# A transformer block on one core: a new fixed order for the same instructions, with 75 of them on another engine

## The chip, the cores and the metric

The kernel runs on one core of a Trainium2 chip. The core has five engines that run side by side, each with its own queue that it works off in order: TensorE for matmuls (PE in the profile, PEld for its weight loads), VectorE (DVE), ScalarE (ACT), GpSimd (POOL) and SyncE (SP), which here only issues DMAs. Engines wait for one another by semaphores. The metric is the device time of one execution in microseconds; a kernel's figure is the median of its runs.

## The reference

One block of a conditioned transformer on 2048 tokens of width 640, in bfloat16. Six rows of 640 numbers come from `silu(c) @ w_mod`: shift, scale and gate for either half.

```python
h = _layernorm(x) * (1 + ca) + sa
x = x + ga * A(h)        # attention: 32 heads of 20, causal, window of 256 keys, then @ wo
h = _layernorm(x) * (1 + cb) + sb
x = x + gb * B(h)        # (sigmoid(h @ w_gate) * (h @ w_up)) @ w_down, inner width 1536
```

## The kernel before

The 2048 tokens are worked in 8 chunks of 256 tokens (two blocks of 128 rows). For each chunk `a` these steps follow one another:

- `ln1`: load x, layer norm statistics on DVE (L776, L778), the inverse root on POOL (L781, L783), the normalised x on DVE (L796) or POOL (L793). It is transposed to hT by PE for chunks 0 to 2 and by a DMA on SP (L803) for the rest; hT then gets scale and shift (the "modulation", L811 on ACT, L812 on DVE or POOL; L857, L858 where it is evacuated from PE's transpose).
- `qkv`: hT times wqkv, in runs of five matmuls of 480 columns into one PSUM bank M; the result is cast out by ACT (L893) or DVE (L894) into stg (queries and keys) or V. stg is transposed to QT and KT, by PE in chunks 0 and 1, by DMAs on SP after that.
- `attention`: in each of two halves of the heads, five sets of scores (three in chunk 0). A set writes the one score tile S, four PSUM banks; ACT takes exp of it into E (L1015), and S can be written again only then. POOL sets the entries outside the window to zero (L1040). Then a burst of PV matmuls (E times V, L669) into a pair of M banks, and `norm` on DVE (L1082 to L1091): transpose, divide by the sum, transpose back. The result goes through DRAM (`doc`) and comes back as oT. A PV burst is issued together with a score set of the next half.
- `outproj`: oT times wo, added to x (L1164), a second layer norm, and h2T by DMA transposes with modulation.
- `mlp`: for six pairs of 128 columns each, ten matmuls for the gate (wg) and ten for the up projection (wu), each into one M bank; tanh on ACT (L1209, out: sig) frees the gate's bank, the product on DVE (L1211, out: hh) the other. Then hh times wd ("down"), added to x (L1230), and out.

The gates ga and gb are not applied to the results: wo and wd are scaled by them (L1253, L1192, out<-in `wd<-wd,gbc`) once the gate's row has been spread over the partitions through DRAM (`gate<-gq`, `gbc<-gate`).

All matmuls of these steps stand on two helper lines: L668 for full tiles, L669 for scores and PV, which use parts of the array.

What sets the order: the build first lists 2121 operations (`Prog.op`), each with its dependencies. The list `PRIO` then gives each operation a number. `schedule` goes through the operations in the order of these numbers; a number's remainder by 5 names the engine:

```python
for o in sorted(self.ops, key=lambda x: x.prio):
    e = ENGS[o.prio % 5]      # ("pe", "act", "dve", "pool", "sp")
```

So `PRIO` fixes each engine's queue. Tiles (buffers) are handed out on the way: of a pool's free buffers an operation takes the one that comes free earliest by the durations written in the program. M has 4 banks, S one, E five buffers. `emit` then puts a semaphore wait ahead of every operation whose inputs or buffer come from another engine.

Of the kernel before, what the change touches and what calls it, by code (L numbers as in the profile page):

```python
# [25 lines left out]
SWITCH = 0.095  # L26
ENGATTR = {"pe": "tensor", "act": "scalar", "dve": "vector", "pool": "gpsimd", "sp": "sync"}
ENGS = ("pe", "act", "dve", "pool", "sp")
OVERLAP = {"pe": 0.0, "act": 0.085, "dve": 0.075, "pool": 0.045, "sp": 0.0}
# [52 lines left out]
class Prog:  # L82
# [69 lines left out]
    def schedule(self):  # L152


        free = {e: START for e in ENGS}
        bw = 0.0
        lastturn = False
# [4 lines left out]
        pemode = 0  # L162
        portend = 0.0
        freed = {}

        def slot_time(pool, s):
            ten = pool.tenant[s]
            if ten is None:
                if not all(x.done for x in pool.init[s]):
                    return None  # L170
                return max([x.end + x.lat for x in pool.init[s]], default=0.0)
            return None if ten.left else freed[ten]

        def take(t, s):
            ten = t.pool.tenant[s]
            t.prev = list(t.pool.init[s]) if ten is None else list(ten.rel)
            t.slot = s
            t.pool.tenant[s] = t

        for o in sorted(self.ops, key=lambda x: x.prio):  # L180
            assert all(d.done for d in o.deps), o.tag
            e = ENGS[o.prio % 5]
            assert e in o.engs, (o.tag, e)
            o.eng = e
            st = max([o.tmin, free[e] + (SWITCH if e == "pe" and o.mode != pemode else 0.0)]
                     + [d.end + (0.0 if d.eng == "pe" and e == "pe" else d.lat) for d in o.deps])
            if o.isdma and e == "sp":
                st = max(st, bw - QMAX)
            for t in o.tiles:
                if t.slot is None:  # L190
                    step = 1 if t.mate is None else 2
                    best = None
                    for s in range(0, len(t.pool.tenant), step):
                        rts = [slot_time(t.pool, s + k) for k in range(step)]
                        if None not in rts and (best is None or max(rts) < best[0]):
                            best = (max(rts), s)
                    assert best is not None, (o.tag, t.name)
                    if t.mate is None:
                        take(t, best[1])
                    else:  # L200
                        take(t, best[1] + t.odd)
                        take(t.mate, best[1] + 1 - t.odd)
                for x in t.prev:
                    st = max(st, x.end + x.lat)
            if e == "dve" and o.port:
                st = max(st, free["pool"])
            elif e == "pool":
                st = max(st, portend)
            o.start = st
            if e == "pe":  # L210
                pemode = o.mout
            dur = o.dur[e]
            free[e] = st + dur - OVERLAP[e]
            if e == "dve" and o.port:
                portend = free[e]
            if o.isdma:
                turn = o.dlat > 3.0
                if e == "sp" and bw - st > 2.0:
                    free[e] += 0.35 if o.dur[e] > 1.0 else 0.1
                bw = max(st + o.dlat, bw + (MIXED if turn != lastturn and bw > st + o.dlat else 0.0)) + o.work  # L220
                lastturn = turn
                o.end = max(bw - 0.83, st + dur)
                s = rr
                rr = (rr + 1) % NDMA
                dmacnt[s] += 16
                o.key, o.val = f"d{s}", dmacnt[s]
                if dmalast[s] is not None:
                    o.deps.append(dmalast[s])
                dmalast[s] = o
            else:  # L230
                o.end = st + dur
            order[e].append(o)
            o.done = True
            for t in o.tiles:
                t.left -= 1
                if t.left == 0:
                    last = {}
                    for x in t.ops:
                        if x.isdma:
                            last[x] = x  # L240
                    for e2 in ENGS:
                        xs = [x for x in t.ops if x.eng == e2 and not x.isdma]
                        if xs:
                            last[e2] = max(xs, key=lambda x: x.start)
                    t.rel = list(last.values())
                    freed[t] = max(x.end + x.lat for x in t.rel)
        self.order = order
        self.span = max(o.end for o in self.ops)
# [88 lines left out]
def c_pe(n):  # L337
# [3 lines left out]
PE_EPS = 0.14  # L341
PRIO = [
# [142 lines left out]
QMAX = 4.5  # L485
# [821 lines left out]
```

## Time and profile before

| | |
|---|---|
| median of 3 runs | 325.76 us (325.64 to 326.33) |
| span of the profiled execution, first to last instruction | 324.3 us |
| median less this span | 1.46 us |
| TensorE busy | 317.3 us, 98% of the span |
| VectorE, ScalarE, GpSimd busy | 211.8, 212.3, 187.2 us |
| granted TensorE clock | 1.000 |

The profiled execution is one of its own; no device time beside its span is listed for it, so the 1.46 us stand for what lies around a span.

How to read it: the rows name the line, the engine, the operation, the tile written and the tiles read, the shape and the count. In a timeline each row has its start and its length in us, like instructions in a row being merged into one (xcount), and in brackets the idle time of the engine just before, with the instruction that ended it. A matmul's shown length holds the time it spends in the array, so lengths of neighbours overlap; what one more matmul costs is seen from longer rows: a row of 15 matmuls of 480 columns takes 3.21 us and one of 9 takes 2.00, so one more costs 0.2. SPq and ACTq are DMA issues, whose length is that of issuing.

### The profile page before, as it was taken

What the parts mean: (1) busy time and instruction counts of PE and PEld (TensorE: products, weight loads), DVE (VectorE), ACT (ScalarE), POOL (GpSimd) and SP (SyncE); (2) the same over time, 40 slices, a digit from 0 to 9 for tenths busy, and PEclk for the clock granted to TensorE, in tenths of its full rate; (3) what the DMA queues carried; (4) which work ended last, traced back from release to release, by engine and by line L of the source; (5) the groups of instructions that cost most, each with busy time, mean ns of one, the idle gap of its engine ahead of it and who ended that gap; (6) DMA issues with size and microseconds to landing.
All of it is one profiled execution on the core that took longest, in us unless ns stands there. A gap on an engine that the chain in (4) does not pass through costs nothing.

```text
span 324.3 us, 11594 instructions
## 1 busy us (share of the span) xinstructions
PE 317.3 (98%) x4872; PEld 222.7 (69%) x4873; DVE 211.8 (65%) x424; ACT 212.3 (65%) x316; POOL 187.2 (58%) x276
## 2 busy tenths in 40 slices
PE   8999999989999999999999999999999999999997
PEld 3564545446776568765776467877786788787885
DVE  5797898778687959674477475837463769264332
ACT  1899985889876687788687867786767764011120
POOL 5128869976668694847585939382939691012100
DMA  7998799989891383824405394340213032202101
GB/s 249 371 333 299 165 269 180 200 137 183 260 164 22 83 109 77 152 61 101 85 22 82 97 103 110 92 69 5 81 40 88 3 79 53 76 20 64 40 2 40
DMA packets 71694, 37.85 MB, mean 117 GB/s; under 512 B 45274, under 2 KB 70362, under 8 KB 71642
## 3 DMA queue, kind: packets, MB, share of 16 engines
q1 hardware_dynamic: 69616, 35.31, 48.3%
q10 hardware_dynamic: 2026, 1.80, 2.1%
q8 instruction: 38, 0.62, 0.8%
q14 instruction: 14, 0.11, 0.1%
HBM read 21.30 MB, written 5.25 MB: 82 GB/s over the span
## 4 chain that ended last, share of the span: by engine, by line
PE 73%; DMA 2%; SPq 2%; DVE 1%; POOL 1%; issue 0%; DVEq 0%
PE M L668 61%; PE S L669 6%; PE M L669 5%; DMA gbc<-gate 2%; SPq L803 2%; DVE wd L1192 1%; POOL x L793 0%; POOL st L788 0%; DVE hh L1211 0%; POOL E L1040 0%; DVE x L1230 0%; DVEq L310 0%
## 5 line engine op out<-in xcount | busy, mean ns | idle before, releaser
L1040 POOL TENSOR_SCALAR_AFFINE_SELECT E<-E 128x512 bf16<-128x512 bf16 (+1 forms) x176 | 142.6, 836 | 68.7 <-ACT E L1015 67.0
L1015 ACT ACTIVATE E<-S 128x512 bf16<-128x512 f32 (+2 forms) x184 | 150.9, 878 | 47.4 <-PE S L669 46.5
L668 PE MATMUL M<-wqkv,hT 128*128 128x480 bf16 (+1 forms) x340 | 73.9, 355 | 0.6 <-ACT hT L846 0.5
L668 PE MATMUL M<-h2T,wu 128*128 128x256 bf16 x480 | 68.0, 273 | 0.5 <-DVE hh L1211 0.5
L668 PE MATMUL M<-h2T,wg 128*128 128x256 bf16 x480 | 67.8, 273 | 0.0
L668 PE MATMUL M<-wd,hh 128*128 128x320 bf16 (+2 forms) x396 | 58.1, 295 | 0.0
L1209 ACT ACTIVATE sig<-M 128x512 f32<-128x512 f32 x48 | 28.9, 602 | 44.1 <-PE M L668 41.7
L1211 DVE SCALAR_TENSOR_TENSOR hh<-sig,M 128x512 bf16<-128x512 f32 x48 | 32.4, 681 | 37.1 <-ACT sig L1209 24.0
L668 PEld LDWEIGHTS M<-h2T,wu 128*128 128x128 bf16 x480 | 45.9, 98 | 8.4 <-issue 1.2
L668 PEld LDWEIGHTS M<-h2T,wg 128*128 128x128 bf16 x480 | 45.7, 98 | 7.1
L668 PEld LDWEIGHTS M<-wqkv,hT 128*128 128x128 bf16 x340 | 30.1, 98 | 27.6 <-DMA wqkv<-in_A_wqkv_dram 1.6
L668 PEld LDWEIGHTS M<-wd,hh 128*128 128x128 bf16 x396 | 36.8, 98 | 14.3 <-DVE hh L1211 0.2
L669 PEld LDWEIGHTS S<-QT,KT 20*64 20x64 bf16 (+1 forms) x1856 | 19.9, 100 | 21.3 <-ACT E L1015 12.0
L1230 DVE TENSOR_TENSOR x<-M,x 128x320 bf16<-128x320 f32 (+2 forms) x33 | 15.6, 476 | 27.2 <-PE M L668 27.2
L669 PE MATMUL S<-QT,KT 20*64 20x256 bf16 (+5 forms) x1856 | 32.1, 228 | 1.2 <-ACT E L1015 1.2
L776 DVE BATCH_NORM_STATS2 st<-x 128x6 f32<-128x320 bf16 x64 | 28.6, 477 | 2.3 <-DMA x<-in_A_x_dram 1.9
L1082 DVE STREAM_TRANSPOSE T<-M 128x512 f32<-128x512 f32 x32 | 21.5, 698 | 9.2 <-PE S L669 8.0
L668 PE MATMUL M<-wo,oT 128*128 128x320 bf16 x160 | 25.4, 299 | 0.0
L669 PE MATMUL M<-E,V 128*32 128x128 bf16 (+1 forms) x960 | 22.8, 246 | 0.8 <-ACT E L1015 0.4
L781 POOL TENSOR_SCALAR st<-st 128x2 f32<-128x2 f32 x16 | 3.7, 234 | 33.8 <-DVE st L778 33.6
L669 PEld LDWEIGHTS M<-E,V 128*32 128x32 bf16 x960 | 19.2, 97 | 5.3 <-issue 2.9
L1091 DVE STREAM_TRANSPOSE On<-Tn 128x1024 bf16<-128x1024 bf16 x16 | 19.8, 1240 | 0.3
(77 smaller groups left out, 240.2 us busy)
## 6 DMA issues: line engine op xcount, KB each, us to landing
x<-in_A_x_dram SPq DMA_DIRECT2D x23, 160.0 KB, 2.3
doc<-On SPq DMA_DIRECT2D x56, 40.0 KB
wd<-in_B_w_down_dram SPq DMA_DIRECT2D x4, 480.0 KB
wd<-in_w_mod_dram SPq DMA_DIRECT2D x5, 320.0 KB
wqkv<-in_A_wqkv_dram SPq DMA_DIRECT2D x4, 400.0 KB
wu<-in_w_mod_dram SPq DMA_DIRECT2D x5, 320.0 KB
oT<-doc SPq DMA_DIRECT2D x8, 192.0 KB, 2.5
out_dram<-x SPq DMA_DIRECT2D x9, 160.0 KB
```

The source lines that it names most:

```text
L668: return e.matmul(o, l, r, start=st, stop=sp, skip_group_check=True)
L669: return e.matmul(o, l, r, start=st, stop=sp, tile_position=tp, skip_group_check=True)
L776: A("dve", lambda e, g, bi=bi, j=j: e.bn_stats(v(bi * 12 + j * 6, 6), src[bi].ap[:, j * 320:(j + 1) * 320]), 0.48, reads=[src[bi].r()], wr ...
L781: A("pool", lambda e, g: e.tensor_scalar(v(28, n), var(), EPS, None, op0=ALU.add), 0.2, reads=[st.r(("m", bi)) for bi in range(n)], writes ...
L803: return e.dma_start_transpose(dst(), src())
L1015: A("act", lambda e, eng: e.activation(dst(), src(), ACT.Exp, scale=SM_SCALE), c_act(n), reads=[Sp.r()], writes=[E.r(key)], prio=3, tag=f" ...
L1040: A("pool", lambda e, eng: e.affine_select(rows(dst), rows(src), pattern=[[0, 8], [sign, n]], compare_op=ALU.is_ge, fill=0.0, base=base, c ...
L1082: A("dve", lambda e, g, h=h: e.transpose(T1.ap[:, 512 * h:512 * h + 512], X[h].ap), 0.694, reads=[X[h].r()], writes=[T1.r(h)], prio=3.5, t ...
L1091: A("dve", lambda e, g: e.transpose(On.ap[:], Tn.ap[:]), 1.22, reads=[Tn.r()], writes=[On.r()], prio=4, tag=f"tr2_{a}")
L1209: A("act", lambda e, g, pg=pg, sg=sg: e.activation(sg.ap[:], pg.ap[:], ACT.Tanh, scale=0.5), c_act(512), reads=[pg.r()], writes=[sg.r()], ...
L1211: A("dve", lambda e, g, pu=pu, sg=sg, f0=f0: e.scalar_tensor_tensor(out=hh.ap[:, f0:f0 + 2, :], in0=sg.ap[:].rearrange("p (a b) -> p a b", ...
L1230: A("dve", lambda e, g, ps=ps, bi=bi, c0=c0, n=n: e.tensor_tensor(x1[bi].ap[:, c0:c0 + n], ps.ap[:, 0:n], x1[bi].ap[:, c0:c0 + n], op=ALU. ...
```

## The change

`PRIO` gets new numbers, and a list `SLOTS` names the buffer of each of 709 tiles, in place of the choice by durations. `schedule` loses the model of durations that chose the buffers. No operation is added, removed or altered.

```diff
-                    step = 1 if t.mate is None else 2
-                    best = None
...
+                    s = SLOTS[tiles[t]] if SLOTS else 0
+                    ten = t.pool.tenant[s]
...
 PRIO = [
-    23, 28, 258, 8, 43, 33, 958, 18, 1448, 38, 3, 507, 513, 72, 67, 48, 53, 58, 76, 84, 101, 99, 144, 149, 154, 159,
+    23, 28, 258, 8, 43, 33, 718, 18, 1218, 38, 3, 507, 513, 72, 67, 48, 53, 58, 76, 84, 101, 99, 144, 149, 154, 159,
...
+SLOTS = [
+    0, 1, 3, 2, 0, 0, 0, 1, 0, 2, 0, 1, 3, 0, 1, 2, 3, 0, 0, 1, 0, 2, 0, 0, 3, 1, 0, 4, 5, 1, 3, 2, 2, 3, 2, 1, 3,
...
```

Sorted by their numbers, the lists say this. The first 140 operations are the same, on the same engines. SP's queue of 193 operations is the same, the 18 DMAs on ACT's queue keep their order, and the 79 operations with scores or PV keep theirs among themselves on PE. Of PE's 907 operations 613 have another place in its queue, by at most 19 places. 75 operations change engine: evacuations of queries, keys and values between ACT and DVE (20 to DVE, 15 to ACT), evacuations of QT, KT and hT between the same two, modulations among ACT, DVE and POOL, and one scaling of wd from POOL to DVE. By engine, before and after: PE 907 and 907, ACT 333 and 331, DVE 424 and 433, POOL 264 and 257, SP 193 and 193.

Some stretches, decoded (number of matmuls in brackets; a number behind a name is the chunk):

```
PE, gaps ahead of the 12th to the 15th of the 79 operations with scores or PV (| is such an operation)
before  q3 k3 (15) | v2 v3 (9)     | v3 q2 v2 (15) | q2 k2 v2 (11) PV
after   q3 k3 (12) | q3 v3 v2 (12) | v3 q2 v2 (13) | q2 v2 k2 (13) PV

PE, the five gaps between scores that end with the second PV of chunk 1
before  q3 wo k3 (14) | k3 q3 wo (11) | q3 wo (10) | q4 (12) | q4 (8) PV
after   q3 wo    (10) | wo       (15) | q3 k3 (10) | q4 (12) | q4 (8) PV

PE, gaps with the first MLP (u: up, g: gate, first chunk), up to the first PV of chunk 2
before  k4 v4 u(4) | g u (20) | g u (24) | g u (44) PV
after   v4 k4 u(2) | g u (20) | g u (20) | g u (52) PV

PE, first PV of chunk 0
before  score | q1 q1 qtr q1 | PV | q1 qtr q1 | score
after   q1 q1 qtr q1 | score | PV | q1 q1 qtr | score

DVE, around the second gate's scaling of wd
before  hh, wd, wd, wd, wd, hh, hh, hh, wd, wd, wd, wd
after   hh, stg, V, wd, hh, wd, statistics, hh, wd, wd, hh, wd, statistics, wd

DVE, ahead of the second PV of chunk 0 (chunk 2's hT, chunk 1's QT)
before  hT, gq, T, QT, QT, hT, hT, hT, gq, T
after   hT, gq, T, QT, hT, hT, T, hT, gq      (the other QT and one hT on ACT)

DVE, second layer norm of chunk 0
before  x, x, stg(4), stg(4), divide
after   x, stg(4), stg(4), x, divide          (the second stg's matmuls: before the 1st score of chunk 2, now behind it)

ACT, exps (e) of chunk 1's last two score sets and chunk 2's first
before  e e | hT hT hT hT e e | stg(4) e e
after   stg(3) e e | hT hT e hT hT e | stg(4) e e
```

More of the change, by code (lines that the diff above doesn't have):

```diff
@@ L152, in schedule @@
     def schedule(self):
-        free = {e: START for e in ENGS}
-        bw = 0.0
-        lastturn = False
         order = {e: [] for e in ENGS}
@@ L161, in schedule, with number @@
         rr = 0
[L162 to L178, printed above, removed]
+        tiles = {}
+        def number(t):
+            if t is not None and t not in tiles:
+                tiles[t] = len(tiles)
+                number(t.mate)
+        for o in self.ops:
+            for t in o.tiles:
+                number(t)
         for o in sorted(self.ops, key=lambda x: x.prio):
@@ L184, in schedule @@
             o.eng = e
[L185 to L188, printed above, removed]
             for t in o.tiles:
                 if t.slot is None:
-                    step = 1 if t.mate is None else 2
-                    best = None
[L193 to L215, printed above, removed]
-            if o.isdma:
[L217 to L223, printed above, removed]
-                rr = (rr + 1) % NDMA
[L225 to L231, printed above, removed]
+                    s = SLOTS[tiles[t]] if SLOTS else 0
@@ new lines, in schedule @@
+                    ten = t.pool.tenant[s]
+                    assert ten is not None or all(x.done for x in t.pool.init[s]), (o.tag, t.name)
+                    assert ten is None or ten.left == 0, (o.tag, t.name)
+                    t.prev = list(t.pool.init[s]) if ten is None else list(ten.rel)
+                    t.slot = s
+                    t.pool.tenant[s] = t
+            if o.isdma:
+                dmacnt[rr] += 16
+                o.key, o.val = f"d{rr}", dmacnt[rr]
+                if dmalast[rr] is not None:
+                    o.deps.append(dmalast[rr])
+                dmalast[rr] = o
+                rr = (rr + 1) % NDMA
@@ L237, in schedule @@
                     last = {}
[L238 to L244, printed above, removed]
+                    for x in sorted(t.ops, key=lambda x: x.prio):
+                        last[x if x.isdma else x.eng] = x
                     t.rel = list(last.values())
-                    freed[t] = max(x.end + x.lat for x in t.rel)
         self.order = order
-        self.span = max(o.end for o in self.ops)
     def emit(self):
@@ L338, in c_pe @@
     return max(n, 64) / 2400.0 + 0.0027
-PE_EPS = 0.14
 PRIO = [
[3 rows of a table removed]
[3 rows of a table added]
     92, 87, 187, 237, 242, 247, 253, 263, 272, 267, 280, 275, 290, 300, 305, 286, 317, 296, 322, 311, 376, 357, 386,
[1 row of a table removed]
[1 row of a table added]
     541, 495, 501, 665, 677, 480, 485, 491, 565, 570, 576, 545, 551, 630, 652, 525, 555, 561, 625, 660, 681, 685,
[111 rows of a table removed]
[111 rows of a table added]
+]
+SLOTS = [
[20 rows of a table added]
 ]
@@ L466 @@
 DSAFE = 1.5
-START = 0.8
-PORTLAG = 0.05
-MIXED = 0.55
 NPB = 0
```

3 lines of the change are left out of this document (removed), and 247 rows, old and new, of tables (PRIO, SLOTS).

## The prediction

> **What bounds the kernel now.** I read the page first, then TensorE's busy time in seven stretches, then the timelines of the stretches where it is idle.
>
> ```profile
> span 324.3 us, 11594 instructions
> PE 317.3 (98%) x4872; PEld 222.7 (69%) x4873; DVE 211.8 (65%) x424; ACT 212.3 (65%) x316; POOL 187.2 (58%) x276
> ...
> q8 instruction: 38, 0.62, 0.8%
> ```
>
> ```profile
> 0.00:10.30 10.30, 8.35 (x76) 1.00 0.82 272
> 10.30:36.00 25.70, 25.62 (x297) 1.00 0.91 301
> 36.00:61.00 25.00, 24.48 (x421) 1.00 1.06 211
> 61.00:72.00 11.00, 9.43 (x177) 1.00 0.84 164
> 72.00:92.00 20.00, 19.49 (x339) 1.00 1.04 223
> 92.00:270.00 178.00, 177.99 (x3134) 1.00 0.39 76
> 270.00:322.20 52.20, 51.91 (x450) 1.00 0.14 39
> ```
>
> Each row gives a stretch, its length, TensorE's busy time and its clock, which is full throughout. Length less busy time is idle time. The first 10.3 us lose 1.95 us, but belong to the 140 operations that keep their places. After 92 us nothing is lost until the last matmul (the 0.29 us in the last row lies behind it). In between: 0.08 + 0.52 + 1.57 + 0.51 = **2.68 us**. TensorE does the same 4872 matmuls in both kernels, so 2.68 us is all that a new order can take out of visible idle time, while in the 230 us after 92 it can only add some. The change is a bet on the stretch from 36 to 92 us.
>
> [...]
>
> **The change, place by place.** The diff alters no instruction's work. All 193 operations on SP's queue keep their order, and so do the DMAs on ACT's; so do the 79 score and PV operations among themselves on PE. What moves are 613 of 907 PE operations by up to 19 places between those, evacuations and modulations among ACT, DVE and POOL, and the buffer that each tile gets. The idle places are these (bracket: idle time ahead, and what ended it):
>
> ```profile
> 38.23 0.84 PE L669 MATMUL M<-E,V 128*32 128x256 bf16 x32 [0.35 <-DVE hT L858]
> ...
> 42.99 3.21 PE L668 MATMUL M<-wqkv,hT 128*128 128x480 bf16 x15
> 46.13 0.43 PE L669 MATMUL S<-QT,KT 20*64 20x256 bf16 x24
> 46.49 2.00 PE L668 MATMUL M<-wqkv,hT 128*128 128x480 bf16 x9
> 48.66 0.43 PE L669 MATMUL S<-QT,KT 20*64 20x256 bf16 x24 [0.17 <-ACT E L1015]
> ...
> 58.92 0.41 PE L669 MATMUL S<-QT,KT 20*128 20x64 bf16 x32
> ...
> 61.60 0.43 PE L669 MATMUL S<-QT,KT 20*64 20x256 bf16 x24 [0.27 <-ACT E L1015]
> ...
> 64.13 0.43 PE L669 MATMUL S<-QT,KT 20*64 20x256 bf16 x24 [0.30 <-ACT E L1015]
> ...
> 67.91 0.43 PE L669 MATMUL S<-QT,KT 20*64 20x256 bf16 x24 [0.42 <-ACT E L1015]
> ...
> 70.48 1.50 PE L669 MATMUL M<-E,V 128*32 128x128 bf16 x64 [0.42 <-ACT E L1015]
> ...
> 86.54 1.25 PE L668 MATMUL M<-h2T,wu 128*128 128x256 bf16 x10 [0.51 <-DVE hh L1211]
> ```
>
> *Place 1, 86.5 us.* The gate for wd lands late, and DVE, in order, stands behind it:
>
> ```profile
> 77.92 5.14 DMA gbc<-gate
> ```
>
> ```profile
> 80.35 0.69 DVE L1211 SCALAR_TENSOR_TENSOR hh<-sig,M 128x512 bf16<-128x512 f32 x1 [0.94 <-ACT sig L1209]
> 83.16 2.65 DVE L1192 TENSOR_TENSOR wd<-wd,gbc 128x640 bf16<-128x640 bf16 x4 [2.12 <-DMA gbc<-gate]
> 85.72 1.27 DVE L1211 SCALAR_TENSOR_TENSOR hh<-sig,M 128x512 bf16<-128x512 f32 x2
> ```
>
> Before, four scalings of wd (2.65 us, 0.66 each) run ahead of the second hh product; the bank that this frees is what PE waits for, from 86.03 to 86.54. After, one scaling stands ahead of that product: 83.16 + 0.66 = 83.8. Its tanh ends at 83.93 (83.34 + 0.59, row below), so it ends near 84.6 instead of 86.4. PE asks no sooner: the 90 matmuls of projection and MLP that lie ahead of the waiting one from chunk 4's keys on are 68 and 22, split by the last score there; after, 62 and 28. The wait has a margin of 86.0 − 84.6 = 1.4 us and goes: **−0.51**. It returns only if the gate lands over 1.4 us later. The scalings pushed back are needed by the down projection alone, which follows the whole first MLP.
>
> *Place 2, 38.2 us.* PV waits for a bank that DVE's hT evacuations free. Before, two QT evacuations stand ahead of those on DVE; after, one, the other having gone to ACT, and one hT evacuation each way changes engine. One such QT evacuation is 2.1/3 = 0.7 us:
>
> ```profile
> L894 DVE CAST QT<-M 128x512 bf16<-128x512 f32 x3 | 2.1, 686 | 1.1 <-PE M L668 1.1
> ```
>
> That covers the 0.35. But ACT's copy now runs behind the exps there, next to a score that reads QT. Between 0 and −0.35 I take **−0.2**.
>
> *Place 3, 48.7 us.* Three of the 15 matmuls ahead of the score at 46.13 move behind it (12 and 12 instead of 15 and 9, 0.2 us each by the quoted rows). A stg evacuation leaves ACT just ahead, so the earlier score finds ACT free. 0.6 us of work covers 0.17 of wait: **−0.17**.
>
> *Place 4, 58 to 70.5 us.* Over half of the idle time: 0.27 + 0.30 + 0.42 + 0.42 = 1.41 us. S has one buffer, so each score waits for the exps of the one before. ACT:
>
> ```profile
> 59.49 2.06 ACT L1015 ACTIVATE E<-S 128x512 bf16<-128x512 f32 x4 [0.72 <-PE S L669]
> 62.14 1.94 ACT L1015 ACTIVATE E<-S 128x512 bf16<-128x512 f32 x2 [0.59 <-PE S L669]
> 63.97 2.07 ACT L811 ACTIVATE hT<-hT,mA 128x256 bf16<-128x256 bf16 x4
> 65.93 1.92 ACT L1015 ACTIVATE E<-S 128x1536 bf16<-128x1536 f32 x2
> ...
> 83.34 0.59 ACT L1209 ACTIVATE sig<-M 128x512 f32<-128x512 f32 x1
> ```
>
> Score to score is 61.60 − 58.92, then 2.53, 3.78, 2.57 us: exps of 1.94 to 2.06, about 0.6 of hand-over, and in the third gap four modulations (2.07). The new order leaves all four on ACT, only mixed with the exps, and PE the same 55 matmuls spread otherwise over the five gaps that end at 70.48. Two extra evacuations on ACT fall into its idle 0.72 and 0.59. A loop that ACT closes isn't shortened: **0**, between −0.3 (an evacuation fewer beside the modulations) and +0.5 (one that misses its gap).
>
> *Place 5, 25 to 30 us.* A score of chunk 0 goes four operations back, to directly ahead of the first PV: one change of PE's mode fewer (161 for 162). Its second exp now waits for PV, which frees an E buffer:
>
> ```profile
> 28.29 1.02 ACT L1015 ACTIVATE E<-S 128x1024 bf16<-128x1024 f32 x1 [0.29 <-PE M L669]
> ```
>
> After, it waits for the first exp (1.02) of the later score instead, some 0.2 us longer at most, with projections as cover. **0**, between −0.2 and +0.3.
>
> *The rest, 92 to 322 us.* PE waits for nothing here before. What could make it wait is the same loop, if too few matmuls lie between two scores. The seven thinnest gaps before hold about ten 480-column matmuls (2.0 to 2.1 us at 0.2 us each); the new order has three such gaps, so it is no tighter. **0**, between 0 and +1.5, nearer to 0 for this reason.
>
> **Sum:** −0.51 − 0.2 − 0.17 = −0.88 us, span 323.4. The shown runs have a median of 325.76 (325.64 to 326.33), 1.46 over the profiled span; start and end are unchanged, so I keep 1.46: **324.9 us**.
>
> **Rivals.**
>
> *A. Nothing measurable.* (0.2%, 0.65 us, is about what a measurement of this kernel tells from no change.) PE that gets to the loop at 56 us sooner still needs QT and KT from SP's unchanged queue, and waits there instead; places 2 and 3 are given back. A new wait of 0.2 somewhere in 230 us does the rest: −0.51 + 0.2, 325.4. Against it: before 56 us PE waits for no such transfer. The change's own aim may also be empty: instruction fetches are 0.62 MB in 38 packets, 0.8% of the DMA engines' time, and no PE wait is put down to them.
>
> [...]
>
> *B. Slower: h2T and the gate come late.* The second normalised x of the first chunk moves behind two stg evacuations on DVE, and the matmuls of the second of them behind the score at 67.91. Those end near 67.91 + 0.43 + five times 0.2 = 69.4, the evacuation (0.7) at 70.1, x at 70.5 instead of 68.0, and SP, in order, stands on its transpose:
>
> ```profile
> 67.24 0.80 DVE L796 TENSOR_SCALAR x<-x,st 128x640 bf16<-128x640 bf16 x2 [1.15 <-POOL st L783]
> ...
> 74.88 0.84 DVE L812 TENSOR_SCALAR h2T<-h2T,scB,shB 128x256 bf16<-128x256 bf16 x3
> ```
>
> ```profile
> 68.06 2.55 SPq L803 DMA_TRANSPOSE h2T<-x  x2
> ...
> 72.35 1.23 SPq L803 DMA_TRANSPOSE hT<-x  x1
> 73.62 4.26 SPq L803 DMA_TRANSPOSE KT<-stg  x1
> ```
>
> ```profile
> h2T<-x SPq DMA_TRANSPOSE x16, 2.6
> ```
>
> ```profile
> 76.82 0.60 PE L668 MATMUL M<-h2T,wu 128*128 128x256 bf16 x4
> ```
>
> The second transpose is issued at 69.3 now (68.06 + half of 2.55) and at 70.6 then, +1.3, and lands at 73.2 instead of 71.9. The modulations that quoted row stands for begin near 74.2 behind an evacuation and end at 75.7; the first MLP matmul is at 76.8. So 2.3 + 1.1 = 3.4 us of delay are hidden, and 1.3 alone costs nothing: this is why the forecast holds. The point is passed if one more transpose on SP is held as KT's was (4.26 us against 1.23, +3.0): 1.3 + 3.0 − 3.4 = 0.9 on PE at 77 us. The gate stands behind it in SP's queue and lands 3.0 late, 1.4 of it covered by place 1's margin and 0.9 by PE's own delay: another 0.7. 324.9 + 1.6 = 326.5.
>
> *C. More goes.* Place 4 gives 0.3 and place 2 its 0.35 on top: 324.4; if all idle time went, 323.1.
>
> **Chances.** The forecast and C, faster by over 0.2% (under 325.1): 0.50, of which C 0.1. A, and smaller losses against the gains: 0.20. B, or 1.5 us of waits after 92 us (326.4): 0.30. The range goes from between C's two times, 323.5, to B's with the 0.5 of place 4 on top, 327.0. The likeliest case alone is 324.2 to 325.1.
>
> **What would show it.** Right: no idle time of PE behind hh near 86 us; four waits still there between 58 and 71, of 1.1 to 1.7 us together; none after 92 us. Wrong: a wait for h2T near 77 us (B); the loop's gaps shorter than exps plus 0.6 us (C); any waits of over 0.5 us together after 92 us, since I rest on there being none; span and median moving apart.

## The result and the profile after

The changed kernel takes **329.99 us** (median of six runs, 328.57 to 333.20) where the kernel before takes 325.76 (325.64 to 326.33): ratio 1.0148, 95% interval 1.0108 to 1.0187, **slower by 1.5%**. The forecast was 324.9 with a range to 327.0. The profiled execution took 329.32 us. Line numbers are 34 lower than before (L669 is now L635, L894 is L860, L1230 is L1196); the kernels of the experiments shift them by another few lines.

The head of the page of the changed kernel:

```profile
span 327.5 us, 11573 instructions
...
PE 317.6 (97%) x4873; PEld 221.4 (68%) x4873; DVE 217.7 (66%) x433; ACT 213.4 (65%) x314; POOL 182.6 (56%) x269
```

TensorE is busy as long as before (317.6 for 317.3), and the span is 3.2 us longer, so what was added is idle time. VectorE's nine extra instructions are not what costs 3 us by their length: it has 66% for 65%. The same seven stretches as in the prediction, TensorE alone (length, busy time, clock):

```profile
0.00:10.30 10.30, 7.74 (x77) 1.00 0.84 278
10.30:36.00 25.70, 25.04 (x286) 1.00 0.98 297
36.00:61.00 25.00, 24.37 (x428) 1.00 0.96 201
61.00:72.00 11.00, 8.65 (x108) 1.00 0.97 170
72.00:92.00 20.00, 20.00 (x396) 1.00 0.90 225
92.00:270.00 178.00, 176.98 (x3075) 1.00 0.40 75
270.00:325.40 55.40, 54.81 (x523) 1.00 0.16 47
```

From 10.3 to 36 us 0.66 us are idle where 0.08 were; from 61 to 72 us 2.35 where 1.57 were; from 72 to 92 nothing where 0.51 was; and in the long stretch where TensorE had waited for nothing, 1.02. The rows that carry it, from TensorE's timelines:

```profile
23.34 1.84 PE L634 MATMUL M<-wqkv,hT 128*128 128x480 bf16 x8 [0.45 <-DVE hT L824]
...
38.81 0.84 PE L635 MATMUL M<-E,V 128*32 128x256 bf16 x32 [0.26 <-DVE hT L824]
...
65.32 2.81 PE L634 MATMUL M<-wqkv,hT 128*128 128x480 bf16 x12 [0.53 <-DVE stg L860]
...
70.97 1.19 PE L634 MATMUL M<-wqkv,hT 128*128 128x480 bf16 x5 [1.75 <-DVE stg L860]
...
94.26 0.39 PE L634 MATMUL M<-h2T,wu 128*128 128x256 bf16 x2 [0.59 <-DVE T L1048]
...
151.42 0.78 PE L634 MATMUL M<-wqkv,hT 128*128 128x480 bf16 x3 [0.29 <-DVE x L1196]
```

By the profile every one of these ends on VectorE. For five of the six the end times agree: TensorE's row starts 0.06 to 0.15 us after the named instruction has ended. The 0.53 us at 65.32 are another matter. That matmul waits for a semaphore of ScalarE as well, and it starts 0.10 us after ScalarE's second modulation of hT has ended:

```profile
64.14 1.09 ACT L777 ACTIVATE hT<-hT,mA 128x256 bf16<-128x256 bf16 x2
```

The same 0.10 us lie there in all eight experiments that have the changed order and its engines at this place (e1, e2, e3, e6, e8, e9, e11, e14), whatever VectorE does meanwhile; in e3 no evacuation of VectorE has ended for 0.3 us before. So this wait is ScalarE's. By the lists ScalarE does the modulations 542, 545, 544, 543 in the old order and 545, 542, 544, 543 in the new one: what TensorE starts behind was the first of the four and is now the second. Before, TensorE waited 0.11 us here, and started 0.10 us behind that modulation's end as well. Below it is called the wait for hT at 65 us, whatever the profile puts it down to.

Before, the waits between 58 and 71 us ended on ScalarE's exps. One of this kind is left, 0.31 us at 59.16. What stood on VectorE ahead of the 1.75 us is in its own timeline:

```profile
65.20 0.32 DVE L860 CAST V<-M 128x160 bf16<-128x160 f32 x1
69.50 0.49 DVE L742 BATCH_NORM_STATS2 st<-x 128x6 f32<-128x320 bf16 x1 [3.97 <-DMA x<-in_A_x_dram]
69.91 0.43 DVE L762 TENSOR_SCALAR x<-x,st 128x640 bf16<-128x640 bf16 x1
70.26 1.22 DVE L860 CAST stg<-M 128x480 bf16<-128x480 f32 x2
71.39 0.92 DVE L762 TENSOR_SCALAR x<-x,st 128x640 bf16<-128x640 bf16 x1
```

VectorE does nothing for 3.97 us: the next operation in its queue is the first statistic of a block of x of chunk 6, and that block has not landed. Behind it stand the normalised x of the first chunk and the two evacuations whose banks TensorE needs. The load is SP's:

```profile
63.59 0.42 SPq L536 DMA_DIRECT2D x<-in_A_x_dram  x1
...
70.37 3.17 SPq L769 DMA_TRANSPOSE h2T<-x  x2
```

It is issued at 63.59 and the statistic can start at 69.50. In the old order this statistic came at 102.8 us. It is one of the moves that the new order makes in VectorE's queue; it is no part of any place that the prediction priced.

### The profile page after: what moved, and what is told of

Read it like the earlier page. It is cut to its first block, busy times and chain, and to the rows that moved or that the text cites. A ratio compares the mean times of both kernels' runs of the same rounds, so it can differ in the third digit from the quotient of the medians.

```text
span 327.5 us, 11573 instructions
## 1 busy us (share of the span) xinstructions
PE 317.6 (97%) x4873; PEld 221.4 (68%) x4873; DVE 217.7 (66%) x433; ACT 213.4 (65%) x314; POOL 182.6 (56%) x269
## 4 chain that ended last, share of the span: by engine, by line
PE 80%; POOL 7%; DVE 6%; issue 2%; ACT 2%; DMA 2%; SPq 1%; DVEq 0%; POOLq 0%; ACTq 0%
PE M L634 67%; PE S L635 7%; PE M L635 6%; POOL E L1006 5%; DMA wd<-in_w_mod_dram 2%; ACT E L981 2%; POOL st L749 1%; DVE wd L1158 1%; DVE x L762 1%; DVE hT L824 1%; DVE T L1048 1%; DVE stg L860 1%; SPq L536 1%; POOL st L747 0%; DVE st L742 0%
## 5 line engine op out<-in xcount | busy, mean ns | idle before, releaser
L634 PE MATMUL M<-wqkv,hT 128*128 128x480 bf16 (+1 forms) x340 | 73.5, 355 | 3.6 <-DVE stg L860 2.3
L634 PE MATMUL M<-h2T,wu 128*128 128x256 bf16 x480 | 70.0, 273 | 0.7 <-DVE T L1048 0.6
L634 PEld LDWEIGHTS M<-h2T,wu 128*128 128x128 bf16 x480 | 44.9, 98 | 9.0 <-DVE T L1048 1.1
L635 PEld LDWEIGHTS S<-QT,KT 20*64 20x64 bf16 (+1 forms) x1856 | 19.9, 100 | 20.1 <-ACT E L981 10.7
L635 PE MATMUL S<-QT,KT 20*64 20x256 bf16 (+5 forms) x1856 | 32.0, 228 | 0.3 <-ACT E L981 0.3
L1196 DVE TENSOR_TENSOR x<-M,x 128x320 bf16<-128x320 f32 (+2 forms) x33 | 15.7, 477 | 24.7 <-PE M L634 24.2
L635 PE MATMUL M<-E,V 128*32 128x128 bf16 (+1 forms) x960 | 22.7, 246 | 0.3 <-DVE hT L824 0.3
L635 PEld LDWEIGHTS M<-E,V 128*32 128x32 bf16 x960 | 19.0, 97 | 4.6 <-issue 1.9
L762 DVE TENSOR_SCALAR x<-x,st 128x640 bf16<-128x640 bf16 x26 | 15.7, 626 | 8.9 <-POOL st L749 8.9
```

The source lines that it names most:

```text
L634: return e.matmul(o, l, r, start=st, stop=sp, skip_group_check=True)
L635: return e.matmul(o, l, r, start=st, stop=sp, tile_position=tp, skip_group_check=True)
L762: return e.tensor_scalar(dst[bi].ap[:], src[bi].ap[:], v(24 + 2 * bi, 1), v(30 + bi, 1), op0=ALU.subtract, op1=ALU.mult)
L1196: A("dve", lambda e, g, ps=ps, bi=bi, c0=c0, n=n: e.tensor_tensor(x1[bi].ap[:, c0:c0 + n], ps.ap[:, 0:n], x1[bi].ap[:, c0:c0 + n], op=ALU. ...
```

## The experiments

The theory that I started from, **S**: this statistic holds VectorE's queue, and that is the loss. Its rival **P**: the loss is many small waits, since the new order puts VectorE's operations where they run longer beside GpSimd's (the 26 normalisations of x take 0.63 us each in its trace, 0.47 before). `put_ahead(names, of)` gives operations a new place in the order, directly ahead of another one, and changes no engine. In the changed kernel the buffers stay too, since `SLOTS` names them; in the kernel before (e4 and e10) they are chosen anew for the order.

To place the losses inside an execution I use one table. For each kernel, TensorE's matmuls are counted at the median start-to-start time of their kind, and at equal amounts of work done the start time in the kernel before is subtracted from that in the other one. So a column that grows by 0.7 between two stretches has lost 0.7 us there. The first column is run-to-run difference of the opening, which is the same in all kernels. Each row is one execution, and since the kinds of matmul follow one another in another order, a column is good to about 0.3 us.

```
us in before:      16.4   63.3   73.5   80.5   87.5   95.5  110.1  161.7  272.2
after               0.2    0.6    1.6    1.6    0.9    1.7    1.7    2.3    2.9
e3 one stat back    0.3    0.7    0.4    1.1    0.4    1.4    1.5    2.1    2.7
e4 before + stat    0.8    0.7    0.7    0.7    0.0    0.0    0.0    0.0    0.0
e5 before, after    0.2    0.2    0.2    0.2   -0.5   -0.5   -0.1    0.6    1.2
e6 e3, before       0.1    0.4    0.1    0.1   -0.6    0.7    0.8    0.8    0.8
e7 before, masks    0.7    1.0    1.0    1.0    0.3    0.3    0.3    0.3    0.3
e8 e3, masks        0.3    0.7    0.8    0.7    1.2    2.2    2.2    2.2    2.5
e10 before, hh     -0.2   -0.3   -0.3   -0.3   -1.0   -0.9   -0.9   -0.9   -0.9
```

**e1, the changed kernel again**, on the chip of e2 to e4. No edit.

> The changed kernel once more, unaltered. If its places of waiting are fixed by the order, the 1.75 us of TensorE's wait near 69 us and VectorE's 3.97 us behind the load of x are there again, within 0.5 us, and the median is 329 to 331. If they belong to the one profiled execution, they are elsewhere or gone.

Measured: 330.60 us (327.46 to 332.07), before 325.84; ratio 1.0132 (1.0072 to 1.0191). The wait for stg is 2.00 us in its profile, and VectorE's for the load 3.71, so these places come from the order. Its spread is wide: two of its four runs had a mean clock of 1.00 (327.46, 329.68) and two of 0.995 (331.52, 332.07); see the last section.

**e2, all four early statistics of chunk 6 put back, and e3, only the one.**

```diff
+put_ahead((886, 885, 882, 883), 884)    # e2
```

```diff
+put_ahead((886,), 884)                  # e3
```

> The changed kernel with the four layer-norm statistics of chunk 6 put back to just ahead of their aggregation. Theory S (VectorE stands behind the statistic of a block of x that has not landed, and the evacuations behind it hold TensorE): TensorE's 1.75 us near 69 us go, VectorE's wait for the load goes from 6.6 to under 3 us, and the median falls by 1.5 to 2.5, to 327.5 to 328.5. Rival P (many small waits from the new order, VectorE held by GpSimd): under 0.7 us are gained, 329.3 or more.

> The changed kernel with only the first of those four statistics put back. Theory S: the same as with all four within 0.5 us, 327.5 to 328.5, since the first one waits and the others find the load landed. If the other three cost as much, 329 or more.

Measured: e2 329.02 (ratio 1.0109, 1.0071 to 1.0148), e3 328.77 (1.0076, 1.0052 to 1.0100). In both the 1.75 us become 0.45, so S holds for its own place. What the place costs is less plain. The medians of e1 and e3 are 330.60 − 328.77 = 1.8 us apart, but with four runs each and e1's spread that alone is not clear of noise. All ten runs of the changed kernel (the result's six and e1's four) have a mean of 330.5, the ten with the statistic put back (e3 and e9) one of 328.6: 1.9, with an interval of 0.5 to 3.3. The clock divides these 1.9: the six runs at a mean clock of 1.00 have a mean of 329.2, only 0.6 above, the four at 0.995 one of 332.4, 3.9 above. The table says the same of executions at full clock: the changed kernel is 1.2 behind e3 at 73.5 us and 0.2 at the end, because e3 has waits that the later TensorE is spared (0.54 for h2T at 79, 0.70 for sig at 89). So the place takes its price in the executions in which the clock falls, and gives most of it back in the others.

Nor is S the loss: e3 is still 328.77 − 325.84 = 2.9 us above the kernel before, and above the 328.5 that S allowed. And e2 shows how tight the queue is: seven statistics put one behind the other bring a wait that the changed kernel doesn't have, again behind VectorE.

```profile
104.54 0.72 PE L643 MATMUL M<-wd,hh 128*128 128x320 bf16 x4 [1.01 <-DVE x L1205]
```

**e4, the kernel before with that one statistic early.**

```diff
+put_ahead((886,), 380)
```

> The kernel before with that one statistic put where the change has it, ahead of the normalised x of chunk 0's second layer norm. Theory S: VectorE waits 2 to 4 us for the load near 65 us, TensorE waits 1.5 to 3 us more between 64 and 80 us, and the median is 327.3 to 328.8 for 325.8. Rival P: 325.5 to 326.4.

Measured: 325.85 (325.22 to 328.82), ratio 1.0016 (0.9989 to 1.0043): no difference in the median, though 3 of its 10 runs took 328.0 to 328.8. Its trace has no new wait of TensorE. The forecast of S, 327.3 to 328.8, is missed by the median. Evacuations of stg stand behind the statistic here too. But in the profile VectorE waits only 0.95 us for this load, which lets the statistic start 4.5 us after its issue; in the changed kernel it is 5.9 us, VectorE gets there 1.2 us sooner, and it waits 3.97. How dear an early statistic is thus depends on when the load lands in the execution. Whether the three longest runs are ones with a late load, no profile shows.

**e5 and e6, one order spliced onto the other.** The lists are those of the two kernels, cut at operation 792 (about 110 us), engines with them, and the buffers chosen for the spliced order; e6 has e3's repair in its first part. The kernels hold the lists written out, here and in e12 to e14; the lines say how they are made.

```diff
+first = by_rank(PRIO_BEFORE)[:792]                 # e5; e6: PRIO_E3
+order = first + [i for i in by_rank(PRIO_AFTER)    # e6: PRIO_BEFORE
+                 if i not in first]
```

> The first 792 operations (to about 110 us) stand in the order and on the engines of the kernel before, all later ones in the changed kernel's. No early statistic of chunk 6 is in it. Theory Q (what is left of the loss without that statistic, 3 us, is a sum of small PE waits at separate places on either side of 110 us: about 1.4 before, 0.5 at 147 to 155, 0.2 near 220, 0.3 at 260 to 273, 0.3 behind the last matmul): 327.0, with the 0.29 us wait for L1205's x near 150 in the trace and none between 74 and 92 but hh's. Rival O (the loss of the rest is one place in the MLP of 74 to 96 us and the clock behind it): 325.8. Rival H (it lies in the second half, where the order of matmul kinds differs): 328.5.

> The reverse: the changed kernel's first 792 operations, with the statistic of chunk 6 put back behind the modulation as in e3, then the order and engines of the kernel before. Theory Q: 325.8 and 1.4, so 327.2, with the waits of 0.53 and 0.45 for stg at 65 and 69 us and the ones of 0.5 to 0.7 between 78 and 92 in the trace and none after 110. Rival O: 328.5, as e3. Rival H: 326.0. Theory Q also says that e5 and e6 above before add up to what e3 is above before.

Measured: e5 327.14 (ratio 1.005, 1.0031 to 1.0069) and e6 326.99 (1.0044, 1.0026 to 1.0063), against 325.79. That is 1.35 + 1.20 = 2.55 of e3's 2.9: what is left without the statistic lies on both sides of 110 us and adds up, as theory Q said; O (one place) and H (second half alone) fall. The table shows where: e6 loses between 87 and 95 us, e5 at about 110, 150 and 266 us. (That both are at −0.5 or −0.6 at 87.5 us is no gain of theirs; e10 below has the reason.) Up to 87 us e6 is level with the old order: its waits for hT at 65 us and for stg at 69 (0.53 and 0.45) come in place of the waits for exps.

The later part is best read on VectorE and GpSimd. First VectorE in e5:

```profile
263.64 1.89 DVE L768 TENSOR_SCALAR x<-x,st 128x640 bf16<-128x640 bf16 x2 [1.99 <-POOL st L755]
265.46 0.34 DVE L1059 RECIPROCAL Dr<-T 128x32 f32<-128x32 f32 x1
265.72 0.62 DVE L1183 SCALAR_TENSOR_TENSOR hh<-sig,M 128x512 bf16<-128x512 f32 x1
```

and GpSimd in e5:

```profile
263.57 1.79 POOL L1012 TENSOR_SCALAR_AFFINE_SELECT E<-E 128x512 bf16<-128x512 bf16 x2
```

Two normalisations of x take 1.89 us while two masks run, and hh comes behind them. The kernel before had at this place, on VectorE:

```profile
262.68 0.77 DVE L796 TENSOR_SCALAR x<-x,st 128x640 bf16<-128x640 bf16 x1 [2.07 <-POOL st L783]
263.36 0.67 DVE L1211 SCALAR_TENSOR_TENSOR hh<-sig,M 128x512 bf16<-128x512 f32 x1
263.95 0.43 DVE L796 TENSOR_SCALAR x<-x,st 128x640 bf16<-128x640 bf16 x1
```

One beside a mask (0.77), hh between, and the other when the masks are over (0.43). hh's own time is the same beside a mask as without (0.67, 0.62). The sum over a kernel, from the groups of instructions by form, before and then after (count, busy us, mean ns):

```profile
L796 DVE TENSOR_SCALAR x<-x,st 128x640 bf16<-128x640 bf16 x26 | 11.3, 466 | 11.3 <-POOL st L783 11.3
```

```profile
L762 DVE TENSOR_SCALAR x<-x,st 128x640 bf16<-128x640 bf16 x26 | 15.7, 626 | 8.9 <-POOL st L749 8.9
```

The same 26 instructions take 4.4 us more. The rows show x slower beside masks (0.77 us for 0.43 alone, 1.89 for two in e5) and hh not (0.67 and 0.62); why the one and not the other, no run shows.

**e7 and e8, the masks cut short**, in the kernel before and in e3. Every instruction and wait stays; two of the three masks work on one row of eight, so part of the masking is left out.

```diff
-            rows = lambda unit: ev(E, unit, (384, 8), (1, n))
+            r = 8 if tag == "far" else 1
+            rows = lambda unit: ev(E, unit, (384, r), (1, n))
...
-... affine_select(..., pattern=[[0, 8], [sign, n]], ...
+... affine_select(..., pattern=[[0, r], [sign, n]], ...
```

> [...] Both theories: DVE's normalisations stay near 0.45 us each; the time is that of before less the waits that end on a mask, 325.0 to 325.8.

> e3 (the changed kernel with the one statistic back) with the same masks cut, so that part of the masking is left out. Theory C (VectorE's operations that take twice as long beside GpSimd's masks are what makes the small waits): the 26 normalisations fall from 16.6 us to about 12.1, the four-fold run of wd scalings to 0.55 us each, the waits at 78, 91 and 150 go, and the time is within 0.8 us of e7's. Rival D (the waits come from the order of the queues, whatever an operation takes): the operations get shorter, but the time stays 2.3 to 3.0 us above e7's.

Measured: e7 326.02 (forecast 325.0 to 325.8; before 325.79), e8 327.34 (ratio to before 1.0049, 1.0028 to 1.0069). The two are 1.3 us apart where before and e3 are 2.9: between the 0.8 of theory C and the 2.3 of D. The groups by form of e8:

```profile
L771 DVE TENSOR_SCALAR x<-x,st 128x640 bf16<-128x640 bf16 x26 | 11.6, 470 | 9.2 <-POOL st L758 8.1 <-DMA hT<-x 1.1
```

and its VectorE at the place near 264:

```profile
264.86 0.80 DVE L771 TENSOR_SCALAR x<-x,st 128x640 bf16<-128x640 bf16 x2 [1.62 <-POOL st L758]
```

0.80 for the two that took 1.89 in e5, in the same order. Near 146 us it is likewise: VectorE waits as long for GpSimd's st as in e3 (0.52 and 0.53 us), but then the two x take 1.12 for 1.89 us and the Tn behind them 0.81 for 1.29, and the wait for x at 151 us is gone. So what matters there is the length of VectorE's operations, and not that GpSimd is free sooner. The table says which part went: from 110 to 272 us e8 loses 0.35, e3 and the changed kernel 1.2. So **most of the later part is VectorE's longer operations beside the masks**. The early part is not. These waits before 95 us stay in e8 (its profile is of its slowest execution, 328.9):

```profile
65.91 2.81 PE L643 MATMUL M<-wqkv,hT 128*128 128x480 bf16 x12 [0.99 <-DVE stg L869]
...
87.68 1.70 PE L643 MATMUL M<-h2T,wu 128*128 128x256 bf16 x14 [0.90 <-DMA wu<-in_B_w_up_dram]
94.73 0.39 PE L643 MATMUL M<-h2T,wu 128*128 128x256 bf16 x2 [0.83 <-DVE T L1058]
```

The first is the wait for hT at 65 us, the second one for a load of wu, which no other trace has; the third, for T, is VectorE's. T stands behind four scalings of wd. In the changed kernel these run beside GpSimd's own scaling, which e8 leaves as it is:

```profile
90.69 2.88 DVE L1158 TENSOR_TENSOR wd<-wd,gbc 128x640 bf16<-128x640 bf16 x4
```

```profile
91.65 1.57 POOL L1158 TENSOR_TENSOR wd<-wd,gbc 128x640 bf16<-128x640 bf16 x1 [1.62 <-DVE wd L1158]
```

In the kernel before they are nearly over when GpSimd begins at 89.87:

```profile
88.49 1.69 DVE L1192 TENSOR_TENSOR wd<-wd,gbc 128x640 bf16<-128x640 bf16 x4
```

So T may be late by longer operations as well (four scalings in 2.88 us in the changed kernel, 1.69 in the one before), with GpSimd's scaling in place of the masks. This is read from the rows; no run tests it.

**e9, e3 with five more places of VectorE's queue mended.** `put_behind` is the reverse of `put_ahead`.

```diff
+put_ahead((886,), 884)
+put_ahead((516,), 375)        # stg ahead of a statistic, 65 us
+put_behind((393,), 428)       # hh ahead of the first wd scaling, 84 us
+put_ahead((829, 830), 400)    # T ahead of two wd scalings, 92 us
+put_behind((1167,), 789)      # x ahead of On, 150 us
+put_ahead((1655,), 1822)      # hh between two normalised x, 264 us
```

> The changed kernel with the statistic of chunk 6 put back as in e3, and five more places of VectorE's queue mended, nothing else: the stg evacuation near 65 us ahead of the statistic of chunk 0 before it (wait of 0.53), hh ahead of the first wd scaling near 84 (the 0.70 for sig behind it), the two transposes T near 92 ahead of the last two wd scalings (0.3 to 0.6), the residual x of L1205 near 150 ahead of the transpose On (0.29), and hh near 264 between the two normalised x (0.12, and about 0.3 that follows). Theory Q (the rest of the loss is these waits, one by one): 328.8 less about 1.8, so 327.0, with none of the five waits in the trace above 0.2. Rival M (VectorE is behind as a whole there, by its twice as long operations beside GpSimd, so that a wait mended comes back at the next thing it makes): 328.3 or more, with as many waits at new places.

Measured: 328.65 (328.01 to 329.36), ratio 1.0089 (1.0074 to 1.0103). Nothing is won against e3's 328.77, as rival M said of the time. TensorE in e9:

```profile
23.84 3.66 PE L653 MATMUL M<-wqkv,hT 128*128 128x480 bf16 x17 [0.80 <-DVE hT L843]
...
66.26 2.81 PE L653 MATMUL M<-wqkv,hT 128*128 128x480 bf16 x12 [0.53 <-DVE stg L879]
...
88.89 0.61 PE L653 MATMUL M<-h2T,wu 128*128 128x256 bf16 x4 [0.55 <-ACT sig L1194]
...
152.86 1.79 PE L653 MATMUL M<-wqkv,hT 128*128 128x480 bf16 x8 [0.80 <-DVE V L879]
```

T near 92 and hh near 267 wait no more. The wait for x at 150 (0.29) is now one of 0.80 for V two microseconds later: VectorE does x sooner and V later. The wait for sig is 0.55 for 0.70. At 65 us nothing could change, since that wait is ScalarE's. So three of the five mends reached their wait, one of them only moved it, and theory Q is refuted for these three at most. The profile is of the slowest of the six runs (329.36) and carries 0.80 us for hT at 23 us, ahead of every mend; from 63 us on it loses 1.4 us by the count of the table, where e3 loses 2.1.

**e10, the kernel before with place 1 of the prediction alone.**

```diff
+put_behind((396, 397), 428)
+put_behind((398,), 440)
```

> The kernel before with place 1 of the prediction alone: hh of L1211 ahead of the wd scalings of L1192 that stood before it (VectorE does one scaling, hh, two scalings, hh, one scaling). Theory as predicted (the wait of 0.51 us at 86 was VectorE's order alone): 325.3, with no wait there. Rival (the wait moves to sig or to the next hh, as 0.70 near 88 in e3 and e6 suggests): 325.8.

Measured: 325.91 (325.12 to 326.75), ratio 1.0010 (0.9999 to 1.0021). The wait is gone from the trace and has come back nowhere near, and the time is the same: the rival's time, but not by its way. The reason is in e5, whose VectorE has the old order at this place:

```profile
82.27 2.27 DVE L1164 TENSOR_TENSOR wd<-wd,gbc 128x640 bf16<-128x640 bf16 x4 [1.04 <-DMA gbc<-gate]
84.47 0.67 DVE L1183 SCALAR_TENSOR_TENSOR hh<-sig,M 128x512 bf16<-128x512 f32 x1
```

The four scalings still stand ahead of hh, and TensorE doesn't wait: the gate landed about a microsecond sooner than in the profile that I had (1.04 us of waiting for it, not 2.12). e4, e5 and e7 all lack the wait, and their columns all fall by 0.7 between 80 and 88 us. The 0.51 belonged to one execution.

**e11, two evacuations put behind the early statistic too**, in the changed kernel.

```diff
+put_behind((516, 517), 886)
```

> The changed kernel, where two evacuations near 65 us (stg, V) are put behind the early statistic of chunk 6 too, so that TensorE stands from 64.6 us until that block of x has landed and both are done, near 70.5. Theory S (VectorE's queue stands behind the load): waits of about 5.5 us there in place of 0.53 and 1.75, and 330 plus 3.3, so 333.3, if the granted clock stays at 1.0. Theory K on the clock (the halved clock of 3.41 us in e1 followed the idle TensorE, and a wait longer than 2 us brings it each time): a stretch of granted clock 0.5 behind the wait in the profile, and 1.7 us more, 335.0. Rival (the halved clock in e1 had nothing to do with the wait): clock 1.00 throughout and 333.3.

Measured: 332.57 (331.56 to 334.13), ratio 1.0215 (1.0187 to 1.0243); the waits are 1.26 and 3.75 us, 5.0 together. That is 2.7 more than the 2.28 of the changed kernel, with a median 2.6 higher, near S's 333.3. But the agreement is partly luck. The 1.26 us are the wait for hT at 65 us again, longer because the transposes of hT landed later here; the edit reached only the second wait, 3.75 for 1.75. And the clock is in the 2.6: all four runs have a mean clock below 1 (0.989 to 0.995), two of six do in the changed kernel. At 0.995, three runs of e11 have a mean of 332.2 and four of the changed kernel 332.4. Theory K said that the clock falls each time, and here it did; its 335.0 was too high by 2.4, since the 330 that I started from holds the clock's price in some runs already. See the last section.

**e12, the old order with the new engines; e13, the new order (with e3's repair) with the old engines; e14, the changed kernel's stretch from operation 425 to 792 alone.** Open by then was whether the early part comes from the 75 engines or from the order.

```diff
+PRIO = [5 * rank_before[i] + PRIO_AFTER[i] % 5 for i in ...]   # e12
```

```diff
+PRIO = [5 * rank_e3[i] + PRIO_BEFORE[i] % 5 for i in ...]      # e13
```

```diff
+order = first 425 of before, to 792 of e3, rest of before      # e14
```

> The kernel before in its own order of all 2121 operations and with its own buffers, with the changed kernel's engine for the 75 operations that change it, and nothing else (the statistic of chunk 6 stays late, the wd scalings stay ahead of hh). Theory V (what is left of the loss comes from the 75: VectorE gets five more stg evacuations and five more h2T modulations, and is late with the next thing that TensorE needs): 327.8 or more, with TensorE's waits ending on VectorE. Rival W (it comes from the order: normalised x next to each other beside two masks, T behind wd scalings, evacuations behind statistics): within 0.6 us of before, 325.2 to 326.4.

> The reverse: the changed kernel's order and buffers with the statistic of chunk 6 put back as in e3, and the kernel before's engine for the 75. Theory V: within 0.6 us of before, 325.2 to 326.4. Rival W: 328.0 or more, as e3, with the 0.29 us wait for x near 150 in it. If both kernels are about 1.5 us above before, order and engines share it.

> The kernel before up to operation 425 (about 56 us) and from 792 (110 us), and between them the changed kernel's order and engines with the statistic of chunk 6 put back. If the early part of the loss, 1.2 us in e6, lies in the first layer's end and the MLP of 57 to 110 us (the waits of 0.53 and 0.45 for stg, 0.70 for sig, 0.29 for T): 327.0. If it lies in the first 57 us (the wait of 0.2 to 0.8 for hT near 22.7): 326.0.

Measured: e12 350.10 (ratio 1.0747, 1.0711 to 1.0783), e13 342.75 (1.053, 1.0502 to 1.0558), before 325.48. **Neither half alone is the loss**: V and W both fall. Either half by itself costs 17 to 25 us, and together (e3) they cost 2.9. VectorE, ScalarE and GpSimd are busy about as long as before, TensorE 4 us longer, at a mean clock of 0.99; what is added is waiting. e12's head reads:

```profile
PE 321.4 (93%) x4872; PEld 222.7 (64%) x4873; DVE 215.3 (62%) x433; ACT 212.5 (61%) x314; POOL 182.1 (52%) x269
```

An operation's engine and its place in that engine's queue belong together, and neither has a price of its own here. e14 took 327.38 (ratio 1.0049, 1.0033 to 1.0066), on the side of "57 to 110 us", but not cleanly: 0.96 us of its waits lie at the first seam, for V, which neither kernel has there. Its waits for hT at 66 us (0.59), for stg at 71 (0.44) and for T at 94 (0.59) are those of the changed order.

## Why the prediction was wrong

**The step that failed** is "The rest", and with it the list of places to price: "The change is a bet on the stretch from 36 to 92 us", and after that "PE waits for nothing here before. What could make it wait is the same loop", worth 0. I looked for new waits only in the loop of scores and exps, on ScalarE. Most of what came, came from VectorE, whose queue I had read only where TensorE was idle before: 0.45 us for hT at 23 us, 1.75 for stg at 71, 0.59 for T at 94, 0.29 for x at 151. After 92 us TensorE waits 1.0 us, over the 0.5 that I had named as a sign of being wrong. By the table the changed kernel loses 2.0 us from 87.5 us to the end, so the bound of 1.5 for this stretch didn't hold either, and the same neglect ahead of 92 us had no bound at all.

- **The statistic of chunk 6** was nowhere in the sum. It stands in the queue that rival B is about, directly ahead of the first of the two normalised x between which B counts two evacuations. I followed what comes after (transposes, h2T, the gate) and not what is ahead. Its 1.9 us (ten runs against ten) lie mostly in executions in which the clock falls. That price was in no term either.
- **Place 1** (−0.51): the wait is gone, as said, but not by the change alone. It was absent from three executions in the old order too, and its repair is worth nothing in the times (e10, 325.91 for 325.75). I treated one execution's late gate as the kernel's.
- **Place 2** (−0.2): 0.26 is left of 0.35, −0.09. **Place 3** (−0.17): gone, right. **Place 5** (0): right, but 0.45 us for hT came before it, at 23 us.
- **Place 4** (0, to +0.5): the four waits of 1.41 us on ScalarE's exps became 0.31 on an exp, 0.53 on ScalarE's hT and 1.75 on VectorE's stg, 2.59 together. Without the statistic (e3: 0.30, 0.12, 0.53, 0.45) it is 1.40, so the value 0 was right but for the statistic, and by luck: two of the exps' waits did go, and the waits for hT and for an evacuation on VectorE took their room.
- **Rival A**'s mechanism had no part. **Rival B** had the sign (0.30) and the place, but its mechanism didn't act: no wait for h2T near 77 in the changed kernel (e3's execution has one of 0.54). **Rival C** nowhere.
- **The span against the median**: in every run of which both are known the time is 1.7 to 1.9 us above the span of the same execution. The 1.46 was the median less the span of another, somewhat slower execution, so that term was about 0.3 short. After, the median is 2.49 above the profiled span, since the profiled execution is a quick one of a kernel that spreads more.

The account: the statistic 1.9 by means, the rest before 110 us 1.2 and after it 1.35 by medians, together 4.45 of the 4.2 to 4.8 measured. Shown: the statistic's place (e2, e3), the split (e5, e6), and VectorE's longer operations beside the masks as the cause of most of the last (e8). **Open** is which operations make the 1.2 before 110 us. By the table they act between 87 and 95 us, where the waits for sig (0.70) and T (0.29 to 0.59) are, but when e9 took T's wait away the time didn't move. That VectorE is late there as a whole, so that a mend in one place comes back in another, is what e9 suggests (150 to 152 us) and not what it shows for this stretch. Open too is how much of the statistic's price is the clock's, beyond the two profiles that have the clock fall.

## What to carry to other kernels

Of a change of order, list what each engine's queue now does ahead of every operation that the bottleneck waits for, also where it waited for nothing before, and ask of each operation put ahead whether it waits for a load. A wait seen in one execution may be that execution's: before it is counted as a gain, ask what late arrival made it. Compare the releaser that a profile names with the end times of the other engines before mending it: e9 mended an evacuation for a wait that was ScalarE's. Here some of VectorE's operations took longer beside GpSimd's (a normalisation of x 0.77 us beside a mask, 0.44 alone), so the order changed durations too, and not only waits.

## What the runs showed of the hardware

**TensorE's clock fell to half around waits of 2.00 and 3.75 us, and not after one of 1.75.** Windows of e1 (length, TensorE's busy time, clock); its 2.00 us wait ends at 71.55:

```profile
64.00:71.00 7.00, 4.98 (x67) 1.00 1.08 204
71.00:72.00 1.00, 0.45 (x3) 0.97 0.00 0
72.00:75.00 3.00, 3.00 (x48) 0.50 0.56 111
75.00:76.00 1.00, 1.00 (x52) 0.82 0.93 204
```

and of e11, whose wait of 3.75 ends at 73.07:

```profile
71.00:72.00 1.00, 0.00 (x0) 1.00 0.83 172
72.00:75.00 3.00, 1.93 (x5) 0.54 0.27 55
75.00:76.00 1.00, 1.00 (x25) 0.50 0.81 163
76.00:79.00 3.00, 3.00 (x78) 0.50 0.81 229
79.00:92.00 13.00, 13.00 (x192) 1.00 1.03 238
```

In e1 the clock is 0.5 for 3.4 us from 71.9, which costs 1.7 (an estimate, half of these 3.4); in e11 for twice that, from 72.2. The changed kernel's profile, with 1.75 us of wait, shows none of it. Its runs split the same way: four at a mean clock of 1.00 took 328.6 to 330.2 us, two at 0.995 took 333.0 and 333.2. That is more than 1.7 apart, so these two runs lost time elsewhere too, perhaps by longer waits; they have no profile. How long a wait has to be for this, no run shows: 2.00 us of waiting, with 0.53 four microseconds ahead of it, had the halved clock behind it in one execution (e1), and 1.75, with the same 0.53, had not in another (the profiled one of the changed kernel). The mean clock was 0.995 in 4 of the 10 runs of the changed kernel, e1's profiled one among them, and the median depends on how many of the runs fall to it.

**VectorE's normalisation of x took 0.44 us alone and 0.77 beside a mask of GpSimd, up to 1.21.** These are medians over the traces of all sixteen executions: 216 of these instructions had nothing of GpSimd's beside them, 83 had a mask beside at least four fifths of their length. The scalings of wd went from 0.48 to 0.76 in the same way, up to 1.40. Statistics (0.48) and hh (0.69) took the same time either way.
